# A hand-planned attention kernel: ScalarE planned by the pace of its ends, weights loaded later in pieces, any two neighbouring waiting score tiles in one exp, instruction lines asked for ahead

## The chip, the cores and the metric

The kernel runs on one core of a Trainium2 chip. The metric is device time in microseconds (us), the median of several executions; lower is better. TensorE is called PE here (its weight loads PEld), VectorE DVE, ScalarE ACT, GpSimd POOL, and SyncE, which only issues DMAs, SP. PSUM, where PE writes its results, has 8 banks, each 128 partitions by 512 fp32 numbers; they are numbered 0 to 7, and two banks are neighbours when their numbers differ by one.

## What is computed

```python
xn = layernorm(x)                                   # x: 2048 x 512, bf16
q  = (xn @ wq) as 32 heads of 16;  k = xn @ wk;  v = xn @ wv   # one k and v for all heads
s  = softmax(q @ k.T / 4) @ v, heads joined, @ wo   # no mask: every query sees every key
h  = silu(xn @ w1)                                  # 512 x 1792
g  = silu(h @ w2)                                   # 1792 x 512
out = x + s * g
```

## The kernel before, in words

**Work.** The 2048 queries are cut into 4 chunks of 512. Scores are made in *slots*: one slot is 2 heads by 64 keys by 512 queries, it fills one PSUM bank, and PE makes it with 4 matmuls of 64 x 32 weights (line 883). A *group* is 64 slots (4 heads of one chunk); there are 32 groups, so 2048 slots. Each slot's exponential is taken in one of two ways.

- An **A slot** is read by ACT with one exp (line 1578) into a place of `pa_sb`, which has NPA = 21 places. PE then multiplies it with v in 2 matmuls (line 1222). One ACTIVATE may read two slots, if their banks are neighbours and two places of `pa_sb` next to each other are free; this is called a *pair* below.
- A **D slot** is turned by DVE into 16-bit integers that are read as bf16 numbers (line 959), an approximate exponential. Four D slots make a batch; POOL adds three different constants to the integers of a whole batch (line 1144, three instructions for four slots), and PE multiplies all 4 versions with v, 8 matmuls for each slot (line 1222). The four weighted versions together make the approximation good enough.

The two MLP products run between the scores: 56 h jobs (w1, then a tanh on ACT at line 700 and a multiply on DVE at line 701) and 16 z jobs (w2, likewise); the q projections and 12 w jobs (wo; the last four row tiles have their own code at the end) follow the same path. PE works in two lanes of 4 matmuls each, whose row and column tiles don't overlap: scores go to lane 1, products with v to lane 0, and the jobs to whichever is free.

**What sets the order.** The whole order of every engine is written by a planner at build time, a loop that keeps one clock for each engine and always lets the engine with the earliest clock choose its next instruction. It uses a table of costs: `T_AF` (the fixed part of an ACTIVATE, beside 0.8333 ns for a column), `MM` (a round of 4 matmuls), `LAT` (from an engine's end to what another sees), and `FETCH` (the least time between two crossings of a line of 256 PE instructions). On the chip the engines follow these orders and wait on semaphores, so a wrong cost in the plan is not an error; it shows as one engine standing at a semaphore where the plan had it busy.

**Choices near the change.**

- `s_step` (line 1041) decides on lane 1 whether the next slot becomes an A or a D slot. It starts an A slot only while ACT's planned backlog `act_need()` is below `A_HIGH`, and a D slot only while DVE's, `dve_backlog()`, is below `D_HIGH`. `MARGIN` is the number of untouched slots that a group must still have for a new D batch.
- `best_a` (line 999) takes the bank of a new A slot: beside the *last* slot that waits for ACT, if that one has no mate.
- `act_step` (line 1547) chooses ACT's next instruction. It looks at the first `WIDE` = 2 of the waiting slots, in the order in which they were made, and reads both in one exp if both are visible within `PAIR_WAIT` and their banks are neighbours; else it reads the first alone.
- `tensor` (line 174) places a PE instruction. When it crosses a line of 256, it may not start before `FETCH` after the last crossing.
- Loads: SP issues x, wk, wv, wq, then all of w1 (1792 KB), w2 (1792 KB) and wo (512 KB) in the first 10 us (lines 424 to 426), and the rows of x that the output needs (`add_xr`, line 763).
- `can_start` (line 1282) and `start_jobs` (line 1297) start the h, z, q and w jobs by their due place (`pace`, in groups) and by the filling of `pa_sb`. Before xn of the first `4 * MIXJ` row tiles is placed, no such job starts (line 1306).
- D slots start when all 16 pieces of k are written (line 927); `take_ob` (line 1186) takes the bank in which a group's product with v is summed.

Of the kernel before, what the change touches and what calls it, by code (L numbers as in the profile page):

```python
# [18 lines left out]
LN_EPS = 1e-5  # L19
T_ISSUE, T_SWDGE = 450.0, 1000.0  # L20
J_BASE, J_END, MIXJ = 0.1, 1.0, 2
# [4 lines left out]
T_P, T_SH, T_TR, T_AF = 600.0, 600.0, 630.0, 52.0  # L26
T_P64, DV_MIN, T_LIB = 1015.0, 40, 300.0
HOLD_PO = 300.0
# [3 lines left out]
Q_URG = 1.153  # L32
J_SLIP = 1.193
NEXT_OB, OB_SLACK = 6, 500.0
NORM_PRIO, T_DIV = 0, 264.0
A_OPEN = 1
T_MS, V_AT = 500.0, 6
# [9 lines left out]
MM = 216.0  # L47
LINE, FETCH = 256, 3670.0
# [4 lines left out]
MARGIN, MARGIN_END = 23, 23  # L53
WIDE, PAIR_WAIT, GRP_WAIT = 2, 51.21, 348.513
Q_LEAD = 2.838
A_HIGH, D_HIGH, SLACK = 3164.101, 2393.829, 73.705
LEAD, CROWD, FRAG, DB_LOW = 427.04, 0.298, 4.106, 1
RUN, HOLD, PRESS = 6, 1017.195, 22
ROOM = 4
START_Z, START_H, AHEAD, NEAR = 10, 13, 1.45, 15  # L60
CLOSING, URGENT, END_DV = 7, 4.336, 60
STARVED = 561.894
JLATE, JEVAC = 1.901, 1
# [7 lines left out]
class Task:  # L71
# [11 lines left out]
    (PE, AC): 221.0, (PE, DV): 221.0, (PE, PE): SWAP,  # L83
    (AC, PE): 176.0, (AC, DV): 140.0, (AC, AC): 110.0, (AC, PO): 160.0, (AC, SP): 160.0,
# [6 lines left out]
class Planner:  # L91

    def __init__(self):
        self.clk = {e: 0.0 for e in ENGINES}
        self.order = {e: [] for e in ENGINES}
        self.lastw = {}
        self.readers = {}
        self.tasks = {e: [] for e in ENGINES}
        self.mode = None
        self.lane = [0.0, 0.0]  # L100
        self.fed, self.cross = 0, -INF
        self.dma_t = self.acc_t = 0.0
        self.count = 0
        self.last2 = {DV: None, PO: None}
# [69 lines left out]
    def tensor(self, mode, lane, dur, emit, reads, writes, t, after=None, n=8):  # L174
# [9 lines left out]
        if line > self.fed // LINE:  # L184
            t = max(t, self.cross + FETCH)
            self.cross = t
# [125 lines left out]
def bass_recurrent_scan__grouped_kv_mqa__dense_activation_silu__prompt_kernel(  # L312
# [29 lines left out]
    with ExitStack() as es:  # L342
# [50 lines left out]
        def bank(b):  # L393
            return ps[:, b * 512:(b + 1) * 512]
# [178 lines left out]
        def mk_K(c, ka, kb, bk=None):  # L573
# [13 lines left out]
            def consume(jb, op):  # L587
                b = jb.bank
                out = []
                for a in range(2):  # L590
                    dst = kt_sb[:, 0, a, ka * P:kb * P]
                    keys = [("kt", k, a) for k in range(ka, kb)]
                    held = [("ps", b), ("part", 0)]
                    if kb == 1:
                        t = Task(AC, T_AF + 93.0 + 0.8333 * n, lambda g, dst=dst, a=a: g.activation(
                            dst, bank(b)[:, 0:n], ACT.Copy, scale=part_sb[:, 0, a:a + 1]), held, keys, 0, out[-1:] or parts)
# [102 lines left out]
        def gated(b, k, scale, dst, key):  # L699
            t1 = Task(AC, 477.0, lambda a: a.activation(t_sb[:, k, :], bank(b), ACT.Tanh, scale=scale), [("ps", b)], [("t", k)], 0)  # L700
# [17 lines left out]
        def mk_z(tt, pace):  # L718
            c, r = divmod(tt, 4)

            def consume(jb, op):
# [10 lines left out]
                    lambda k, rows: w2_sb[rows, k, :], lambda k: ["w2", ("u", k)])  # L732
# [597 lines left out]
        def do_job(t, jb):  # L1330
            mk, rd, dur = jb.rounds[jb.pos]
            op = pl.tensor(jb.mode, None, dur, mk(jb.bank), rd, [("ps", jb.bank)], t)
# [158 lines left out]
        def pe_step():  # L1491
# [44 lines left out]
            if not t_done and ("ob", 3) in pl.lastw and pl.ready(PE, [("ob", 3)], [("ps", 6)]) <= t:  # L1536
                n = st["warm"] = st.get("warm", 0) + 1
                pl.tensor("F", None, T_COLD if n <= N_COLD else MM, lambda pe: pe.matmul(
                    bank(6), lhsT=zer_sb[:, 0:P], rhs=zer_sb[:, :], start=True, stop=True), [("ob", 3)], [("ps", 6)], t)
# [6 lines left out]

        def act_step():
# [138 lines left out]
```

## Time and profile before

| | before |
|---|---|
| median of 3 executions | 677.74 us (677.01 to 677.88) |
| the profiled execution | 678.45 us |
| its span, first to last instruction | 676.5 us |
| mean granted PE clock | 0.997 |
| largest busy shares | PE 98%, ACT 98%, DVE 93%, POOL 88% |

The profile lists for every engine its busy time and the number of its instructions; groups of instructions by line, with the number, the mean duration of one and what ended the idle time before them; the waits between engines in sum; a table by stretch of the span; and the chain of work that ended last. A duration in the groups reaches from an instruction's start to its own end, and on ACT one instruction starts before the last has ended, so the mean duration (745 ns for a single exp) is not the pace at which they follow each other; that pace is read from the chain, where consecutive pieces of one engine are laid end to end. Likewise PE's busy share is no measure of its load, since matmuls overlap; matmuls per us of a stretch are.

### The profile page before, as it was taken

What the parts mean: (1) busy time and instruction counts of PE and PEld (TensorE: products, weight loads), DVE (VectorE), ACT (ScalarE), POOL (GpSimd) and SP (SyncE); (2) the same over time, 40 slices, a digit from 0 to 9 for tenths busy, and PEclk for the clock granted to TensorE, in tenths of its full rate; (3) what the DMA queues carried; (4) which work ended last, traced back from release to release, by engine and by line L of the source; (5) the groups of instructions that cost most, each with busy time, mean ns of one, the idle gap of its engine ahead of it and who ended that gap; (6) DMA issues with size and microseconds to landing.
All of it is one profiled execution on the core that took longest, in us unless ns stands there. A gap on an engine that the chain in (4) does not pass through costs nothing.

```text
span 676.5 us, 47198 instructions
## 1 busy us (share of the span) xinstructions
PE 666.1 (98%) x21990; PEld 324.4 (48%) x21990; DVE 631.4 (93%) x1144; ACT 659.8 (98%) x1198; POOL 598.2 (88%) x596
## 2 busy tenths in 40 slices
PE   7999999999999999999999999999999999999997
PEld 3445455444444444445344455554445545454443
DVE  8889999999999999998999999999899999999972
ACT  5999999999999999999999999999999999999995
POOL 4028899999989999998999998999799999999981
PEclk9999999999999999999999999999999999999999
DMA  8510000000000000000000000000000001000001
GB/s 298 170 31 4 5 4 5 4 5 4 5 4 21 19 29 12 5 4 5 4 5 4 21 27 28 5 4 5 4 5 4 5 20 36 19 5 5 5 4 34
DMA packets 11733, 14.98 MB, mean 22 GB/s; under 512 B 1809, under 2 KB 10769, under 8 KB 11537
## 3 DMA queue, kind: packets, MB, share of 16 engines
q1 hardware_dynamic: 10928, 10.78, 5.0%
q8 instruction: 172, 2.82, 1.7%
q0 software_dynamic: 320, 0.92, 0.5%
q10 hardware_dynamic: 288, 0.26, 0.1%
q14 instruction: 25, 0.20, 0.1%
HBM read 8.95 MB, written 2.10 MB: 16 GB/s over the span
## 4 chain that ended last, share of the span: by engine, by line
PE 61%; ACT 34%; DVE 3%; issue 0%
PE ps L883 34%; ACT pa_sb L1578 32%; PE ps L652 13%; PE ps L1222 12%; ACT t_sb L700 2%; DVE stats_sb L486 1%; PE ps L1429 0%; PE ps L554 0%; DVE kt_sb L598 0%; DVE xnT_sb L565 0%; DVE xn_sb L515 0%; PE ps L580 0%; DVE v_sb L626 0%; PE ps L617 0%; DVE var_sb L509 0%
## 5 line engine op out<-in xcount | busy, mean ns | idle before, releaser
L1578 ACT ACTIVATE pa_sb<-ps 128x512 bf16<-128x512 f32 (+1 forms) x1107 | 633.5, 804 | 4.6 <-PE ps L883 4.0
L1144 POOL INT64_ADD ds_sb<-db_sb x580 | 589.0, 1039 | 29.5 <-PE ps L1222 16.3
L883 PE MATMUL ps<-qt_sb,kt_sb 64*32 64x512 bf16 x8192 | 566.4, 380 | 3.9 <-ACT pa_sb L1578 1.2
L959 DVE TENSOR_SCALAR db_sb<-ps 128x512 uint16<-128x512 f32 x776 | 487.0, 682 | 17.7 <-PE ps L883 9.9
L1222 PE MATMUL ps<-ds_sb,v_sb 64*32 64x512 bf16 x4656 | 409.5, 377 | 0.0
L883 PEld LDWEIGHTS ps<-qt_sb,kt_sb 64*32 64x32 bf16 x8192 | 184.4, 90 | 267.0 <-ACT pa_sb L1578 163.1
L1222 PE MATMUL ps<-pa_sb,v_sb 64*32 64x512 bf16 x2544 | 308.9, 379 | 0.0
L1222 PE MATMUL ps<-db_sb,v_sb 64*32 64x512 bf16 x1552 | 190.2, 378 | 0.0
L1222 PEld LDWEIGHTS ps<-ds_sb,v_sb 64*32 64x32 bf16 x4656 | 146.3, 91 | 11.6 <-issue 0.6
L652 PE MATMUL ps<-xnT_sb,w_sb 64*32 64x512 bf16 x1792 | 135.7, 378 | 0.1
L652 PE MATMUL ps<-w_sb,u_sb 64*32 64x512 bf16 x1792 | 133.9, 378 | 0.0
L1222 PEld LDWEIGHTS ps<-pa_sb,v_sb 64*32 64x32 bf16 x2544 | 89.0, 91 | 9.5 <-ACT pa_sb L1578 2.7
L1222 PEld LDWEIGHTS ps<-db_sb,v_sb 64*32 64x32 bf16 x1552 | 55.7, 91 | 4.6
L700 ACT ACTIVATE t_sb<-ps 128x512 bf16<-128x512 f32 x72 | 53.1, 737 | 0.0
L652 PEld LDWEIGHTS ps<-xnT_sb,w_sb 64*32 64x32 bf16 x1792 | 42.3, 91 | 17.5 <-ACT pa_sb L1578 2.9
L652 PEld LDWEIGHTS ps<-w_sb,u_sb 64*32 64x32 bf16 x1792 | 43.0, 91 | 14.0 <-DVE db_sb L959 0.8
L701 DVE SCALAR_TENSOR_TENSOR u_sb<-t_sb,ps 128x512 bf16<-128x512 bf16 x56 | 38.0, 678 | 1.0 <-ACT t_sb L700 0.5
L652 PE MATMUL ps<-xnT_sb,wq_sb 64*32 64x512 bf16 x480 | 37.7, 378 | 0.0
L1239 DVE STREAM_TRANSPOSE ps<-ps 128x512 f32<-128x512 f32 (+1 forms) x33 | 23.2, 707 | 13.0 <-PE ps L1222 13.0
L652 PE MATMUL ps<-wo_sb,on_sb 64*32 64x512 bf16 x384 | 31.6, 378 | 0.1
L1268 POOL DMA_DIRECT2D kt_sb<-kt_sb x4 | 2.8, 699 | 27.2 <-DVE mv_sb L490 10.1
L1244 DVE TENSOR_TENSOR otr_sb<-ps,rcp_sb 128x256 bf16<-128x256 f32 (+1 forms) x33 | 13.3, 404 | 0.2
(73 smaller groups left out, 182.6 us busy)
## 6 DMA issues: line engine op xcount, KB each, us to landing
w_sb<-in_B_w_dram SPq DMA_DIRECT2D x2, 1792.0 KB, 13.8
xr_sb<-in_A_x_dram SPq DMA_DIRECT2D x16, 128.0 KB, 2.9
out_dram<-ob_sb SPq DMA_DIRECT2D x16, 128.0 KB, 1.8
ds_sb<-in_A_x_dram SPq DMA_DIRECT2D x3, 512.0 KB, 6.8
kt_sb<-kt_sb POOLq DMA_DIRECT2D x4, 224.0 KB, 2.9
wq_sb<-in_A_wq_dram SPq DMA_DIRECT2D x1, 512.0 KB, 4.9
wo_sb<-in_A_wo_dram SPq DMA_DIRECT2D x1, 512.0 KB, 16.9
ds_sb<-in_A_x_dram SPq DMA_DIRECT2D x2, 128.0 KB, 3.0
```

Source lines behind the costliest of these rows:

```text
L486: ts_ = pl.add(Task(DV, 593.0, lambda v, t=t: v.bn_stats(stats_sb[:, t, :], x_tile(t)), [xkey(t)], [("st", t)], 1 + j, gate=(lambda j=j: S ...
L652: h = pe.matmul(bank(b)[32 * j:32 * (j + 1), :], lhsT=lhs(k, rows, 32 * j, 32), rhs=rhs(k, rows), start=first, stop=last, tile_position=(r ...
L700: t1 = Task(AC, 477.0, lambda a: a.activation(t_sb[:, k, :], bank(b), ACT.Tanh, scale=scale), [("ps", b)], [("t", k)], 0)
L701: t2 = Task(DV, T_P, lambda v: v.scalar_tensor_tensor(out=dst, in0=t_sb[:, k, :], scalar=1.0, in1=bank(b), op0=ALU.add, op1=ALU.mult), [(" ...
L883: h = pe.matmul(bank(b)[32 * j:32 * j + 32, :], lhsT=kt_sb[r0:r0 + 64, g % 2, i, k0:k0 + 32], rhs=qt_sb[r0:r0 + 64, g // 2 % NQR, :], star ...
L959: bt.P[k] = pl.add(Task(DV, T_P, lambda v: v.tensor_scalar(db_sb[:, bt.b, k * NQ:(k + 1) * NQ], bank(b), 128.0 * LOG2E, 128.0 * (SHIFT_BET ...
L1144: whole["po"].append(pl.add(Task(PO, T_P64, lambda g: g.int64_add(ds_sb[:, s, :].bitcast(U64), db_sb[:, bt.b, :].bitcast(U64), words), rea ...
L1222: h = pe.matmul(bank(OB)[q:q + 32, :], lhsT=lhs[rows], rhs=rhs[rows], start=s0, stop=s1, tile_position=(64 * l, q), skip_group_check=True)
L1239: t1 = pl.add(Task(DV, (T_TR - 60.0) / parts + 60.0, lambda v, cols=cols: v.transpose(bank(OB)[:, cols], bank(OB)[:, cols]), [("ps", OB)], ...
L1244: norm["m", g, h] = pl.add(Task(DV, T_DIV / parts + 68.0, lambda v, bl=bl: v.tensor_tensor(o3[:, bl, DH * e:DH * e + DH], f3[:, bl, 0:DH], ...
L1268: kt1[c] = pl.add(Task(PO, T_SWDGE, lambda e: e.dma_start(kt_sb[DH:P, 1, :, cols], kt_sb[0:P - DH, 0, :, cols]), [("kt", k, a) for k in ra ...
L1578: op = pl.place(AC, 0.8333 * NQ * n + T_AF, lambda a: a.activation(pa_sb[:, s * NQ:(s + n) * NQ].rearrange("p (b n) -> p b n", n=NQ), ps3[ ...
```

## The change

The diff does five things, and sets some forty numbers of the planner anew.

1. **Costs.** `T_AF` becomes 63.5, the three places that had costs of their own for ACT use it, `MM` becomes 218, some latencies are changed.
2. **Lines.** A crossing waits for the line's arrival (`come`). A line is asked for when PE is `LOOK` = 68 instructions short of the line before it, and comes `FETCH` after that or after the line before. Jobs count their true number of instructions.
3. **Loads.** w1 is issued behind xn of row tile 5; w2 in four pieces, each behind one of the first h results; wo and the first rows for the output behind later ones.
4. **Pairs.** `best_a` looks for a bank beside *any* waiting slot without a mate; `act_step` pairs any slot that is visible with a neighbour that is visible, out of order, unless the oldest has waited more than `SKIP` = 1500 ns.
5. **Numbers.** Among others `A_HIGH` 3164 to 1583, `D_HIGH` 2394 to 1518, `MARGIN` 23 to 19, `MIXJ` 2 to 3, `PRESS` 22 to 18.

```diff
+W1_AT, SKIP = 5, 1500.0
-J_BASE, J_END, MIXJ = 0.1, 1.0, 2
+J_BASE, J_END, MIXJ = 0.073, 1.084, 3
-T_P, T_SH, T_TR, T_AF = 600.0, 600.0, 630.0, 52.0
+T_P, T_SH, T_TR, T_AF = 600.0, 600.0, 630.0, 63.5
-HOLD_PO = 300.0
+HOLD_PO = 374.374
...
-MM = 216.0
-LINE, FETCH = 256, 3670.0
+MM = 218.0
+LINE, FETCH, FED, LOOK = 256, 3684.358, 58, 68
...
-MARGIN, MARGIN_END = 23, 23
-WIDE, PAIR_WAIT, GRP_WAIT = 2, 51.21, 348.513
+MARGIN, MARGIN_END = 19, 20
+WIDE, PAIR_WAIT, GRP_WAIT = 14, 47.267, 237.034
-A_HIGH, D_HIGH, SLACK = 3164.101, 2393.829, 73.705
+A_HIGH, D_HIGH, SLACK = 1582.599, 1518.392, 43.301
-RUN, HOLD, PRESS = 6, 1017.195, 22
-ROOM = 4
-START_Z, START_H, AHEAD, NEAR = 10, 13, 1.45, 15
+RUN, HOLD, PRESS = 6, 1411.229, 18
+ROOM = 5
+START_Z, START_H, AHEAD, NEAR = 8, 9, 1.03, 17
...
-    (AC, PE): 176.0, (AC, DV): 140.0, (AC, AC): 110.0, (AC, PO): 160.0, (AC, SP): 160.0,
+    (AC, PE): 154.0, (AC, DV): 135.0, (AC, AC): 110.0, (AC, PO): 160.0, (AC, SP): 160.0,
...
         if line > self.fed // LINE:
-            t = max(t, self.cross + FETCH)
-            self.cross = t
+            t = max(t, self.come[line])
+        ahead = (self.fed + n + LOOK) // LINE
+        if ahead == len(self.come) - 1:
+            self.come.append(max(t, self.come[ahead]) + FETCH)
...
-        dma(SP, "w1", w1_sb[:], B_w1.rearrange("(dc p) f -> p dc f", p=P), 1792, ["w1"], prio=2)
-        dma(SP, "w2", w2_sb[:], B_w2.rearrange("(ft p) n -> p ft n", p=P), 1792, ["w2"], prio=3)
-        dma(SP, "wo", wo_sb[:], A_wo.rearrange("(o p) n -> p o n", p=P), 512, ["wo"], prio=4)
+        def later(task, which):
+            task.gate = lambda: which() is not None and which().op is not None
+            task.after = lambda: which().op
...
+        later(dma(SP, "w1", w1_sb[:], w1v, 1792, ["w1"], prio=2), lambda: xn_task.get(W1_AT))
+        for k, (f0, f1) in enumerate(((0, 4), (4, 8), (8, 11), (11, 14))):
+            later(dma(SP, "w2", w2_sb[:, f0:f1, :], w2v[:, f0:f1, :], 128 * (f1 - f0), [("w2", k)], prio=3), hidden(0, k))
+        wov = A_wo.rearrange("(o p) n -> p o n", p=P)
+        later(dma(SP, "wo", wo_sb[:], wov, 512, ["wo"], prio=4), hidden(0, 4))
...
-            t1 = Task(AC, 477.0, lambda a: a.activation(t_sb[:, k, :], bank(b), ACT.Tanh, scale=scale), [("ps", b)], [("t", k)], 0)
+            t1 = Task(AC, T_AF + 0.8333 * NQ, lambda a: a.activation(t_sb[:, k, :], bank(b), ACT.Tanh, scale=scale), [("ps", b)], [("t", k)], 0)
...
+            if tt < 4:
+                later(xr_task[tt], hidden(0, 5))
...
         def best_a(banks, when):
-            u = units[-1] if len(units) > st["expn"] else None
-            if u is not None and not u.mate:
-                near = [b for b in banks if abs(b - u.bank) == 1]
-                if near:
-                    return min(near, key=lambda b: room(when) - room([x for x in when if x != b])), True
+            lone = {u.bank: u for u in units[st["expn"]:] if not u.mate}
+            near = [b for b in banks if b - 1 in lone or b + 1 in lone]
+            if near:
+                b = min(near, key=lambda b: room(when) - room([x for x in when if x != b]))
+                lone[b - 1 if b - 1 in lone else b + 1].mate = True
+                return b, True
...
+        def waiting(t):
+            q = units[st["expn"]:]
+            if not q:
+                return q
+            q = [u for u in q if u.vis <= max(t, q[0].vis) + PAIR_WAIT]
+            at = {u.bank: u for u in q}
+            for u in q:
+                if u is not q[0] and t - q[0].vis > SKIP:
+                    break
+                near = [at[b] for b in (u.bank - 1, u.bank + 1) if b in at]
+                if near:
+                    return [u, min(near, key=lambda v: q.index(v))]
+            return q[:1]
 
         def act_step():
...
-            q = units[st["expn"]:st["expn"] + WIDE]
+            q = waiting(t)
             rx = None
             if q:
-                q.sort(key=lambda u: u.bank) if False else None
-                q = [u for u in q if u.vis <= max(t, q[0].vis) + PAIR_WAIT]
-                while len(q) > 1:
-                    bs = sorted(u.bank for u in q)
-                    if bs[-1] - bs[0] == len(q) - 1:
-                        break
-                    q.pop()
...
             if rx is not None and rx <= t + 25:
+                for u in q:
+                    units.remove(u)
                 q.sort(key=lambda u: u.bank)
+                units[st["expn"]:st["expn"]] = q
```

More of the change, by code (lines that the diff above doesn't have):

```diff
@@ L24 @@
 LOG2E = 1.4426950408889634
[L26 removed]
+T_P, T_SH, T_TR, T_AF = 600.0, 600.0, 630.0, 63.5
 T_P64, DV_MIN, T_LIB = 1015.0, 40, 300.0
[L28 removed]
+HOLD_PO = 374.374
 RSQRT_M = float(0x5F1FFFF9)
 RSQRT_C = ((-0.703952253, 0.703952253 * 2.38924456), (-0.5, 1.5))
[L32 to L34 removed]
+Q_URG = 0.308
+J_SLIP = 1.308
+NEXT_OB, OB_SLACK = 6, 192.595
 NORM_PRIO, T_DIV = 0, 264.0
[L36 to L37 removed]
+A_OPEN = 5
+T_MS, V_AT = 500.0, 7
 T_TP, T_COLD, N_COLD = 56.0, 427.0, 11
@@ L100, in __init__ @@
         self.lane = [0.0, 0.0]
-        self.fed, self.cross = 0, -INF
+        self.fed, self.come = FED, [-INF, -INF]
         self.dma_t = self.acc_t = 0.0
@@ L731, in mk_z @@
             product(jb, lambda k, rows, a, n: u_sb[rows, k, r * P + a:r * P + a + n],
-                    lambda k, rows: w2_sb[rows, k, :], lambda k: ["w2", ("u", k)])
+                    lambda k, rows: w2_sb[rows, k, :], lambda k: [("w2", (k >= 4) + (k >= 8) + (k >= 11)), ("u", k)])
         def scaled(tt, b, r=None):
@@ L1331, in do_job @@
             mk, rd, dur = jb.rounds[jb.pos]
-            op = pl.tensor(jb.mode, None, dur, mk(jb.bank), rd, [("ps", jb.bank)], t)
+            op = pl.tensor(jb.mode, None, dur, mk(jb.bank), rd, [("ps", jb.bank)], t,
+                           n={"F": 2 * NDC * len(jb.arg) if jb.kind == "T" else 8, "H": 64}.get(jb.mode, 8))
             jb.pos += 1
@@ L1538, in pe_step @@
                 pl.tensor("F", None, T_COLD if n <= N_COLD else MM, lambda pe: pe.matmul(
-                    bank(6), lhsT=zer_sb[:, 0:P], rhs=zer_sb[:, :], start=True, stop=True), [("ob", 3)], [("ps", 6)], t)
+                    bank(6), lhsT=zer_sb[:, 0:P], rhs=zer_sb[:, :], start=True, stop=True), [("ob", 3)], [("ps", 6)], t, n=2)
                 return True
```

17 lines of the change are left out of this document (10 added, 7 removed).

## The prediction, made before the changed kernel was run

> **What bounds the kernel now.** I read the header and the shares first. Four engines are nearly full at once, so the table by stretch comes next, to see whether that holds in each stage or only on average; then the groups, for the number of instructions of each kind.
>
> ```profile
> span 676.5 us, 47198 instructions
> PE 666.1 (98%) x21990; PEld 324.4 (48%) x21990; DVE 631.4 (93%) x1144; ACT 659.8 (98%) x1198; POOL 598.2 (88%) x596
> ```
>
> ```profile
> 0.00:17.00 17.00, 13.10 (x239) 6.48 (x243) 14.63 (x78) 9.63 (x19) 7.24 (x13) 0.96 0.90 298
> 17.00:34.00 17.00, 15.99 (x369) 7.72 (x357) 14.56 (x39) 15.86 (x27) 0.66 (x1) 0.94 0.54 168
> 34.00:51.00 17.00, 16.74 (x458) 8.45 (x450) 14.37 (x32) 16.16 (x29) 5.04 (x6) 1.00 0.11 31
> 51.00:100.00 49.00, 48.89 (x1662) 26.05 (x1662) 48.39 (x84) 49.00 (x92) 44.47 (x45) 1.00 0.02 5
> 100.00:200.00 100.00, 99.64 (x3416) 47.79 (x3396) 96.56 (x163) 99.98 (x185) 96.89 (x96) 1.00 0.02 5
> 200.00:300.00 100.00, 99.99 (x3452) 46.11 (x3443) 98.37 (x168) 99.86 (x182) 98.03 (x98) 1.00 0.05 15
> 300.00:400.00 100.00, 99.59 (x3384) 48.08 (x3384) 94.56 (x161) 100.00 (x188) 95.42 (x95) 1.00 0.04 10
> 400.00:500.00 100.00, 99.53 (x3384) 50.17 (x3360) 94.46 (x160) 99.78 (x187) 94.18 (x94) 1.00 0.04 10
> 500.00:600.00 100.00, 99.87 (x3424) 50.59 (x3416) 96.78 (x165) 100.00 (x180) 97.70 (x97) 1.00 0.05 15
> 600.00:640.00 40.00, 40.00 (x1370) 18.01 (x1352) 38.88 (x66) 40.00 (x77) 39.45 (x40) 1.00 0.02 5
> 640.00:660.00 20.00, 20.00 (x662) 9.28 (x656) 15.15 (x25) 20.00 (x31) 16.70 (x17) 1.00 0.02 4
> ```
>
> The columns are stretch, length, then PE, PEld, DVE, ACT, POOL with busy us and number of instructions, the clock, DMA share and GB/s. From 51 to 660 us ACT is busy in every microsecond but a few tenths; DVE and POOL have 2 to 6% left. PE's busy share says nothing, but its count does: 1662 + 3416 + 3452 + 3384 + 3384 + 3424 + 1370 + 662 = 20,754 matmuls in 609 us, 29.34 ns for each, and in its best stretch (200 to 300) 100 us / 3452 = 28.97 ns. The best is only 1.3% ahead of the mean, so PE runs close to a pace of its own.
>
> ```profile
> L1144 POOL INT64_ADD ds_sb<-db_sb x580 | 589.0, 1039 | 29.5 <-PE ps L1222 16.3 <-PE ps L883 9.3 <-DVE db_sb L959 3.3
> L883 PE MATMUL ps<-qt_sb,kt_sb 64*32 64x512 bf16 x8192 | 566.4, 380 | 3.9 <-ACT pa_sb L1578 1.2 <-issue 1.0 <-DVE v_sb L626 0.4
> L1578 ACT ACTIVATE pa_sb<-ps 128x512 bf16<-128x512 f32 x942 | 502.9, 745 | 2.1 <-PE ps L883 1.7
> L959 DVE TENSOR_SCALAR db_sb<-ps 128x512 uint16<-128x512 f32 x776 | 487.0, 682 | 17.7 <-PE ps L883 9.9 <-PE ps L1222 3.5 <-POOL ds_sb L1144 0.8
> L1222 PE MATMUL ps<-ds_sb,v_sb 64*32 64x512 bf16 x4656 | 409.5, 377 | 0.0
> L1222 PE MATMUL ps<-pa_sb,v_sb 64*32 64x512 bf16 x2544 | 308.9, 379 | 0.0
> L1222 PE MATMUL ps<-db_sb,v_sb 64*32 64x512 bf16 x1552 | 190.2, 378 | 0.0
> ...
> L1578 ACT ACTIVATE pa_sb<-ps 128x1024 bf16<-128x1024 f32 x165 | 182.0, 1145 | 2.5 <-PE ps L883 2.3
> ```
>
> The slots are split into 942 + 2 x 165 = 1272 A slots and 776 D slots. An A slot costs PE 4 + 2544/1272 = 6 matmuls, a D slot 4 + (4656 + 1552)/776 = 12. Only 330 of the 1272 A slots share an exp.
>
> How long an exp really holds ACT is in the chain, whose pieces lie end to end:
>
> ```profile
> 349.30 1.83 ACT pa_sb L1578 x2
> 351.13 0.49 ACT t_sb L700
> 351.62 1.47 ACT pa_sb L1578 x3
> 353.09 0.49 ACT t_sb L700
> 353.58 2.45 ACT pa_sb L1578 x5
> ```
>
> Five singles take 2.45 us, 0.49 each; the two of the first row are pairs, 1.83/2 = 0.915 each. So a pair saves 2 x 0.49 - 0.915 = 0.065 us, and I use 0.063, from 0.49 against 512 columns at (0.915 - 0.49)/512 = 0.83 ns: 0.49 - 0.427. The plan before had 0.427 + 0.052 = 0.479 for a single, so it believed ACT 11 ns faster at each of some 1180 instructions, and PE pays for it by standing at banks that ACT has not left yet:
>
> ```profile
> PEld ps L883 <- ACT pa_sb L1578: 163.1, 573, 0.7
> ...
> ACT pa_sb L1578 <- PE ps L883: 4.0, 6, 2.0
> ```
>
> PE's score loads wait 573 times for an exp (163.1 us of the load queue, much of it beside running matmuls), ACT only 6 times for PE. ACT is the bound, PE the second, and PSUM banks are what they meet at.
>
> **The change part by part.** *Pairs* (`waiting`, `best_a`). At least none is added (165 stay); at most all 1272 slots pair, 636. Saving S on ACT: 0 to 471 x 0.063 = 29.7 us. For: half of the 1107 exps end with a score standing behind them, and a pair frees two neighbours at one instant, which then are refilled together. Against: 8 banks, of which the sum and a job take about two and the D slots some more. `D_HIGH` falls by 0.88 us, more than one D slot of 0.68, so about one bank passes to the A slots. Reading out of order also lets the oldest slot stand for up to 1.5 us; what waits for it is its product with v, and at a group's end the sum, so it costs only there: 32 groups, nothing as long as the next group's products are at hand. No row lies near either end, so I take the middle, 400 pairs: S = 235 x 0.063 = 14.8 us.
>
> The Trainium skill, page "ScalarE: Activation LUTs", section "What ACT_TABLE_LOAD costs", gives an ACTIVATE with immediates a fixed 186 ns, of which 93 ns overlap with the next, so 93 ns would go with each pair; by that S would be an estimated 21.9 us. The chain shows 63 ns, and the sum keeps it.
>
> *Costs and lines.* They add no instruction; they change where in PE's order scores, products and jobs stand. With ACT's true pace in the plan PE should be put before a bank that is free. Gain P: nothing, up to PE holding its best stretch's pace in all stretches, 20,754 x (29.34 - 28.97) ns = 7.7 us. Below nothing there is no end of P's own: PE that waits more is the last rival. I take 7.7, since a whole 100 us of the same mixture ran at that pace, with the most D work beside it.
>
> *How S and P become time.* Let d slots go from D to A (which `A_HIGH`, `D_HIGH` and `MARGIN` decide). ACT pays 0.458 us for each (half a pair), PE is spared 6 x 29.34 ns = 0.176 us. With x saved, ACT gives x = S - 0.458 d and PE x = P + 0.176 d. So x = (0.176 S + 0.458 P) / 0.634 = (2.60 + 3.53)/0.634 = **9.7 us**, with d = 11. POOL loses 11 x 0.75 x 1.04 = 8.6 us and DVE 11 x 0.6 = 6.6 of work, about as much as the span, so neither becomes the bound. The ends: S = P = 0 gives 0, S = 29.7 with P = 7.7 gives 13.8.
>
> *Loads.* Which waits could they touch?
>
> ```profile
> w_sb<-in_B_w_dram SPq DMA_DIRECT2D x2, 1792.0 KB, 13.8
> ...
> ds_sb<-in_A_x_dram SPq DMA_DIRECT2D x3, 512.0 KB, 6.8
> ...
> wo_sb<-in_A_wo_dram SPq DMA_DIRECT2D x1, 512.0 KB, 16.9
> ```
>
> ```profile
> 16.21 1.38 DVE L515 TENSOR_SCALAR xn_sb<-ds_sb,mv_sb,rstd_sb 128x512 bf16<-128x512 bf16 x4
> ...
> 27.70 1.05 DVE L515 TENSOR_SCALAR xn_sb<-ds_sb,mv_sb,rstd_sb 128x512 bf16<-128x512 bf16 x3
> ...
> 57.30 0.69 DVE L701 SCALAR_TENSOR_TENSOR u_sb<-t_sb,ps 128x512 bf16<-128x512 bf16 x1
> ```
>
> ```profile
> L652 PE MATMUL ps<-xnT_sb,w_sb x1792: 372/376/388, 22.9 to 582.7; 64*32 64x512 bf16 x200
> ...
> L652 PE MATMUL ps<-w_sb,u_sb x1792: 375/376/388, 106.9 to 657.1; 64*32 64x512 bf16 x200
> ```
>
> w1 behind xn of tile 5 (about 17 us) lands about 31; the first h started at 22.9, but with `MIXJ` = 3 it waits for tile 11 (28.7) anyway, so w1 delays it 2 us more. That moves one or two h jobs of 56 behind the opening, where PE does 369 matmuls in 17 us against 576 at its mean pace: cost nothing, at most two jobs of 32 matmuls, 1.9 us. The four w2 pieces leave behind the first h results; SP then stands at these waits, and behind it on its queue wait the other pieces, wo, the four rows of x and much later the stores. In this trace four h results were there at 58 us, and a piece of 512 KB takes 6.8 us, while the first z is at 106.9: some 40 us of cover. If it were gone, z and its tanh would be late, and other jobs would fill in.
>
> What the pieces may disturb is PE's own instruction supply, which now meets them in the full stretch:
>
> ```profile
> q8 instruction: 172, 2.82, 1.7%
> ```
>
> ```profile
> PEld ps L883 <- issue: 2.6, 8, 0.6
> PEld ps L652 <- issue: 2.6, 7, 0.6
> ...
> PEld ps L1222 <- issue: 0.6, 2, 0.4
> ```
>
> 2.82 MB in 172 packets is 16.4 KB each, one for 43,980/172 = 256 PE instructions. The waits of 51 to 660 us that nothing visible ends are 5.8 us in 17 pieces. Six more loads at most double the longest, 0.6 us, at each: 3.6 us lost, or, since the opening is relieved of 4 MB, something gained. I take 0.
>
> *Ends.* D slots start after the last k. `MIXJ` = 3 takes h work out of DVE's way before that, POOL's first add is at 47 us; the last z may come some tenths earlier. Within 3 us either way; I take 0.
>
> **Sum.** 678.45 - 9.7 = 668.75 on the profiled execution, which lies 0.71 above the median: **668.0 us**.
>
> **The rivals.**
> 1. *PE has room.* If its pace is not its own but ACT's, as the 573 waits say, PE gives way and all of S counts: 677.7 - 14.8 = 663, with more pairs down to 655. For it: ACT is full in all stretches. Against: matmuls per 100 us hardly vary, 3384 to 3452, and there are waits on nothing visible. The Trainium skill, page "Runtime: NRT & Kernel Launch", section "Instruction fetch mechanics", is on its side: fetching is hidden, since instructions leave more slowly than blocks of 256 come. By that the lines would be worth nothing and hold PE back nowhere. The waits of 0.6 us speak against it in part.
> 2. *PE stays as slow as it is.* P = 0: x = 2.60/0.634 = 4.1, 673.6 us. The same place is reached by few new pairs with P whole: 3.53/0.634 = 5.6, 672.
> 3. *It doesn't do what it says.* No bank beside a waiting slot is free, pairs stay near 165, the plan's mistakes elsewhere fill up: 677.7.
> 4. *Slower: ACT starves behind its pairs.* A pair holds two banks for 0.915 us and returns both at once; then two scores at 0.22 us a round, each 0.38 long, must be made before the next pair can be read, with a backlog cut to 1.58 us. ACT's 4.0 us of waiting would grow. The turning point is a mean wait of 14.8/400 = 0.037 us behind each pair. At 0.1 us ACT loses 40 - 14.8 = 25.2 us; shared with PE by the formula (P = 0) that is 0.278 x 25.2 = 7.0: 685 us. Against it: ACT almost never waits today.
>
> **How the numbers follow.** Forecast (666 to 672) 0.42, PE has room 0.25, PE stays 0.17, no effect 0.05, starving 0.11. A measurement of this kernel can tell about 0.2%, 1.4 us. Faster 0.84, same 0.05, slower 0.11. Range 655.0 to 677.0: below it part of the first rival, above it the last two.
>
> **What would show it.** Right: some 400 instructions of 128x1024 at line 1578; A slots near 1283; ACT's waits for PE under 10 us; over 3450 matmuls in each 100 us; fewer than 573 waits for exps. Wrong: pairs under 250; ACT idle by tens of us after pairs; issue waits grown between 45 and 90 us; POOL's first add later than 50 us.

## The result and the profile after

| | before | changed |
|---|---|---|
| median | 677.23 us (676.50 to 678.13, 22 executions) | 674.58 us (671.38 to 677.95, 22 executions) |
| ratio | 1 | 0.9961, interval 0.9951 to 0.9971 |
| the profiled execution | 678.45 us, span 676.5 | 674.70 us, span 672.9 |

So the change is faster by 0.39%, 2.65 us, where 9.7 us were forecast. The direction was right, the size was not: the sum was more than three times too large. The medians also differ in another way, to which the last experiments lead: the changed kernel's executions lie 6.6 us apart, those of the kernel before 1.6.

The changed kernel's shares, its table by stretch and its groups, which answer to the same views of before:

```profile
span 672.9 us, 47414 instructions
PE 660.8 (98%) x22086; PEld 373.0 (55%) x22086; DVE 632.6 (94%) x1158; ACT 653.9 (97%) x1172; POOL 612.1 (91%) x610
```

```profile
100.00:200.00 100.00, 99.87 (x3460) 58.69 (x3451) 98.81 (x169) 99.39 (x183) 99.95 (x99) 1.00 0.02 5
200.00:300.00 100.00, 99.99 (x3500) 55.85 (x3499) 99.62 (x172) 99.90 (x179) 99.17 (x99) 1.00 0.05 15
300.00:400.00 100.00, 99.92 (x3454) 54.37 (x3441) 96.87 (x167) 99.99 (x181) 99.00 (x98) 1.00 0.04 10
400.00:500.00 100.00, 100.00 (x3471) 60.55 (x3461) 96.95 (x167) 99.74 (x183) 97.83 (x98) 1.00 0.04 10
500.00:600.00 100.00, 99.52 (x3442) 56.06 (x3431) 98.03 (x168) 99.33 (x182) 100.00 (x99) 1.00 0.05 15
600.00:640.00 40.00, 39.69 (x1388) 23.46 (x1380) 38.37 (x66) 39.49 (x74) 38.01 (x39) 1.00 0.02 5
640.00:660.00 20.00, 19.02 (x576) 9.04 (x556) 5.96 (x11) 20.00 (x29) 15.96 (x16) 1.00 0.01 3
660.00:672.90 12.90, 7.43 (x150) 2.51 (x138) 4.71 (x13) 5.67 (x9) 0.00 (x0) 1.00 0.13 43
```

PE runs 3442 to 3500 matmuls in each 100 us, before 3384 to 3452. POOL, 94 to 98% busy before, has reached 98 to 100. From 640 us DVE does little (5.96 of 20 us, before 15.15), while ACT is full.

```profile
L1160 POOL INT64_ADD ds_sb<-db_sb x594 | 602.8, 1044 | 12.8 <-DVE db_sb L974 6.2 <-PE ps L1238 4.8 <-PE ps L898 1.6
...
L974 DVE TENSOR_SCALAR db_sb<-ps 128x512 uint16<-128x512 f32 x792 | 493.2, 680 | 10.8 <-PE ps L898 5.9 <-POOL ds_sb L1160 2.0 <-PE ps L1238 1.0
L1605 ACT ACTIVATE pa_sb<-ps 128x512 bf16<-128x512 f32 x906 | 477.5, 694 | 4.9 <-PE ps L898 4.5
...
L1605 ACT ACTIVATE pa_sb<-ps 128x1024 bf16<-128x1024 f32 x175 | 183.0, 1096 | 2.0 <-PE ps L898 1.6
```

Here is where the sum fails: **175 pairs** instead of 400, before 165. A slots are 906 + 2 x 175 = 1256, sixteen fewer than before, not eleven more; D slots are 792. ACT was relieved, by 16 x 0.427 + 26 x 0.063 = 8.5 us, but by giving slots away.

```profile
PEld ps L898 <- ACT pa_sb L1605: 81.9, 336, 0.8
PEld ps L898 <- DVE db_sb L974: 30.4, 136, 0.5
DVE ps L1255 <- PE ps L1238: 16.8, 4, 13.6
```

The score loads wait for exps half as long as before (163.1 us, 573 times), as forecast. Other signs that I had named for a right forecast came too: ACT's exps wait 6.1 us for scores, under 10, and four of the five stretches of 100 us have over 3450 matmuls. But pairs under 250 were a sign of being wrong. DVE's longest wait, in one piece at the end of the span, is 13.6 us; before it was 8.0:

```profile
DVE ps L1239 <- PE ps L1222: 13.0, 7, 8.0
```

The chain of the changed kernel shows what it waits for (start, us, what):

```profile
639.54 9.06 ACT pa_sb L1605 x15
648.60 0.49 ACT t_sb L713
649.09 13.33 ACT pa_sb L1605 x15
662.42 0.04 issue
662.46 0.40 PE ps L1238 x4
```

ACT's exps set the last 23 us before the closing work. DVE has read its last D slot at 644.2 us, before at 657.2; POOL's adds for the D slots go on until 656.0 (the changed kernel's lines, then the one of before):

```profile
643.47 0.69 DVE L974 TENSOR_SCALAR db_sb<-ps 128x512 uint16<-128x512 f32 x1 [0.30 <-PE ps L1238]
638.64 17.33 POOL L1160 INT64_ADD ds_sb<-db_sb  x17 [0.40 <-PE ps L898]
```

```profile
655.27 1.89 DVE L959 TENSOR_SCALAR db_sb<-ps 128x512 uint16<-128x512 f32 x3 [0.71 <-PE ps L883]
```

### The profile page after: what moved, and what is told of

It reads as the page before. It is cut to its first block, busy times and chain, and to the rows that moved or that the text cites. A ratio compares the mean times of both kernels' runs of the same rounds, so it can differ in the third digit from the quotient of the medians.

```text
span 672.9 us, 47414 instructions
## 1 busy us (share of the span) xinstructions
PE 660.8 (98%) x22086; PEld 373.0 (55%) x22086; DVE 632.6 (94%) x1158; ACT 653.9 (97%) x1172; POOL 612.1 (91%) x610
## 4 chain that ended last, share of the span: by engine, by line
PE 74%; ACT 20%; DVE 4%; POOL 1%; issue 0%
PE ps L898 31%; PE ps L1238 26%; ACT pa_sb L1605 19%; PE ps L665 16%; DVE stats_sb L499 1%; ACT t_sb L713 1%; DVE xn_sb L528 1%; POOL kt_sb L461 1%; PE ps L1446 0%; DVE kt_sb L611 0%; DVE xnT_sb L578 0%; DVE v_sb L639 0%; POOL v_sb L459 0%; DVE var_sb L522 0%; DVE var_sb L524 0%
## 5 line engine op out<-in xcount | busy, mean ns | idle before, releaser
L1605 ACT ACTIVATE pa_sb<-ps 128x512 bf16<-128x512 f32 (+1 forms) x1081 | 622.8, 759 | 6.9 <-PE ps L898 6.1
L1160 POOL INT64_ADD ds_sb<-db_sb x594 | 602.8, 1044 | 12.8 <-DVE db_sb L974 6.2
L974 DVE TENSOR_SCALAR db_sb<-ps 128x512 uint16<-128x512 f32 x792 | 493.2, 680 | 10.8 <-PE ps L898 5.9
L1238 PE MATMUL ps<-pa_sb,v_sb 64*32 64x512 bf16 x2512 | 330.7, 377 | 3.0 <-ACT pa_sb L1605 2.3
L898 PEld LDWEIGHTS ps<-qt_sb,kt_sb 64*32 64x32 bf16 x8192 | 197.6, 90 | 190.0 <-ACT pa_sb L1605 81.9
L1238 PEld LDWEIGHTS ps<-ds_sb,v_sb 64*32 64x32 bf16 x4752 | 166.7, 92 | 22.0 <-issue 3.4
L665 PE MATMUL ps<-w_sb,u_sb 64*32 64x512 bf16 x1792 | 140.1, 378 | 0.5 <-issue 0.5
L1238 PEld LDWEIGHTS ps<-pa_sb,v_sb 64*32 64x32 bf16 x2512 | 101.6, 92 | 25.1 <-ACT pa_sb L1605 11.1
L665 PEld LDWEIGHTS ps<-w_sb,u_sb 64*32 64x32 bf16 x1792 | 48.8, 92 | 12.8 <-issue 2.6
L1284 POOL DMA_DIRECT2D kt_sb<-kt_sb x4 | 2.8, 700 | 23.8 <-DVE kt_sb L611 14.6
L665 PEld LDWEIGHTS ps<-xnT_sb,wq_sb 64*32 64x32 bf16 x480 | 11.7, 91 | 4.1 <-DVE db_sb L974 0.7
```

Source lines behind the costliest of these rows:

```text
L665: h = pe.matmul(bank(b)[32 * j:32 * (j + 1), :], lhsT=lhs(k, rows, 32 * j, 32), rhs=rhs(k, rows), start=first, stop=last, tile_position=(r ...
L898: h = pe.matmul(bank(b)[32 * j:32 * j + 32, :], lhsT=kt_sb[r0:r0 + 64, g % 2, i, k0:k0 + 32], rhs=qt_sb[r0:r0 + 64, g // 2 % NQR, :], star ...
L974: bt.P[k] = pl.add(Task(DV, T_P, lambda v: v.tensor_scalar(db_sb[:, bt.b, k * NQ:(k + 1) * NQ], bank(b), 128.0 * LOG2E, 128.0 * (SHIFT_BET ...
L1160: whole["po"].append(pl.add(Task(PO, T_P64, lambda g: g.int64_add(ds_sb[:, s, :].bitcast(U64), db_sb[:, bt.b, :].bitcast(U64), words), rea ...
L1238: h = pe.matmul(bank(OB)[q:q + 32, :], lhsT=lhs[rows], rhs=rhs[rows], start=s0, stop=s1, tile_position=(64 * l, q), skip_group_check=True)
L1605: op = pl.place(AC, 0.8333 * NQ * n + T_AF, lambda a: a.activation(pa_sb[:, s * NQ:(s + n) * NQ].rearrange("p (b n) -> p b n", n=NQ), ps3[ ...
```

## The experiments

Each ratio is to the kernel before, run beside it on the same chip; the chips differ, so the ratios compare better than the times. Where a kernel's number of pairs and A slots is given, it is counted in its program. The kernels of one session were measured beside each other: the four parts on one chip; those on pairs, loads and the end on a second; PE by itself, more_instructions, costs_numbers and other_lead on a third; after_again and the three on lines on that third chip too, but later; the last two on a fourth.

**The parts, one at a time and one left out.** My theory A held that the true costs bring the gain through PE's order; rival B, that the forty numbers do.

only_costs, and its opposite no_costs, which is the changed kernel with these lines as before:

```diff
-T_P, T_SH, T_TR, T_AF = 600.0, 600.0, 630.0, 52.0
+T_P, T_SH, T_TR, T_AF = 600.0, 600.0, 630.0, 63.5
-MM = 216.0
+MM = 218.0
-    (AC, PE): 176.0, (AC, DV): 140.0, (AC, AC): 110.0, (AC, PO): 160.0, (AC, SP): 160.0,
+    (AC, PE): 154.0, (AC, DV): 135.0, (AC, AC): 110.0, (AC, PO): 160.0, (AC, SP): 160.0,
```

> The kernel before with the planner's costs alone corrected (T_AF, MM, the latencies, the three ACT costs). It has 178 pairs and 1268 A slots, before 165 and 1272. Theory A (the gain is PE's order under true costs): P is there almost whole, S is 13 x 0.063 = 0.8 us, so (0.176 x 0.8 + 0.458 x 8)/0.634 = 6, less some us at the end of the span: 672 to 674.5 us; the score loads wait for exps under 120 us in sum, before 163. Rival B (the gain is the forty numbers): within 1 us of before, 677, and the waits as before.

Measured: 1.0026, interval 1.0014 to 1.0038: slower. The score loads do wait less for exps, 91.4 us, but that isn't time.

> The changed kernel with the planner's costs as before (T_AF 52, MM 216, old latencies); all else of the change stays. 152 pairs, 1260 A slots. Theory A: the gain goes, 676 to 678 us, and the score loads wait for exps over 130 us in sum. Rival B: it stays, 674 to 675 us.

Measured: 1.0008, 0.9992 to 1.0025. The gain isn't there, though the score loads wait 117.2 us for exps, not over 130.

only_numbers and no_numbers, the lines of the diff that set numbers alone:

```diff
-A_HIGH, D_HIGH, SLACK = 3164.101, 2393.829, 73.705
+A_HIGH, D_HIGH, SLACK = 1582.599, 1518.392, 43.301
...
```

> The kernel before with the planner's forty numbers of the change alone (A_HIGH, D_HIGH, MARGIN, MIXJ and so on), the costs, lines, loads and pairs as before. 126 pairs, 1264 A slots. Theory A: no gain, 677 us within 1.5. Rival B: most of the gain, 674 to 675 us.

Measured: 1.0011, 1.0001 to 1.0022.

> The changed kernel with the forty numbers as before; costs, lines, loads and pairs of the change stay. 173 pairs, 1260 A slots. Theory A: the gain stays, 673 to 675 us. Rival B: it goes, 677 us.

Measured: 1.0044, 1.0027 to 1.0061.

As measured, both A and B fall: neither part alone is a gain, and without either one the rest is none. The changed kernel itself was not measured on this chip, and after_again below shows that it does not gain on every occasion, so this is not proof. That numbers and costs are fitted to each other is my guess; no_numbers, with the costs of the change and the numbers of before, is the slowest of the four. POOL's idle time before its adds is 24.1, 19.9, 26.1 and 24.1 us in these four, 29.5 before and 12.8 in the changed kernel; but two later executions of the changed kernel have 18.3 and 14.8, so it is no sure mark of it.

One thing mars the kernels that take the numbers without the new pair rule (only_numbers and, below, costs_numbers and costs_numbers_lines). `WIDE` = 14, which the new `act_step` doesn't use, lets the old one read longer runs: 6, 6 and 9 of their exps read three slots.

**Pairs.** no_pairs_at_all and wait_for_mate are the changed kernel with one line each:

```diff
-                near = [at[b] for b in (u.bank - 1, u.bank + 1) if b in at]
+                near = []
```

> The changed kernel with each A slot read by its own exp: 0 pairs, 1248 A slots, 800 D slots. S is -175 x 0.063 = -11.0 us against the changed kernel. By the formula of the prediction with P unchanged: 0.278 x 11.0 = 3.1 us slower, 677.7. If ACT alone set the time: 11.0 less the 8 slots fewer (3.9), 7.1 us slower, 681.7. If pairs were worth nothing (PE or GpSimd the bound): within 1 us of 674.6.

Measured: 1.0036, 1.0019 to 1.0053, against 0.9961 for the changed kernel: 0.75% or some 5 us slower, between the 3.1 of the formula and the 7.1 of ACT alone. On this same chip no_loads has 0.9974 and longer_end 0.9965, whose orders are the changed kernel's, or are it up to the last group; against these it is 4 to 5 us. The 175 pairs are worth their place. (The profiled execution, 674.75 us, was the fastest of its twelve; no size is read from it.)

```diff
-WIDE, PAIR_WAIT, GRP_WAIT = 14, 47.267, 237.034
+WIDE, PAIR_WAIT, GRP_WAIT = 14, 250.0, 237.034
```

> The changed kernel in which ACT waits up to 250 ns for a neighbour instead of 47 (PAIR_WAIT): 282 pairs, 1240 A slots. If only the number of pairs counted, S grows by 107 x 0.063 = 6.7 us: 672.5 us. If pairs can only be had by standing still, each bought pair costs up to 0.25 us of ACT and saves 0.063: up to 107 x 0.19 = 20 us of ACT, shared 0.278 x 20 = 5.6 or more: 680 us or slower, and ACT's waits for PE grow by tens of us.

Measured: 1.0137, 1.0121 to 1.0153: 686.71 us, slower by 1.4% than before, with 282 pairs. ACT pays for them by standing, 18.5 us ahead of the pairs, where the changed kernel has 2.0:

```profile
L1605 ACT ACTIVATE pa_sb<-ps 128x512 bf16<-128x512 f32 x676 | 358.3, 633 | 1.4 <-PE ps L898 1.0
...
L1605 ACT ACTIVATE pa_sb<-ps 128x1024 bf16<-128x1024 f32 x282 | 285.6, 1046 | 18.5 <-PE ps L898 12.4 <-PE ps L1238 1.1 <-PE ps L665 0.2
```

A pair beyond those that come by themselves costs more than the 0.063 us it saves. This is the mechanism of my fourth rival, though the change doesn't set it off, because it waits 47 ns at most.

**Loads.** no_loads issues the weights in the first 10 us again; all compute orders stay the same, so this is the cleanest pair of kernels here.

```diff
-        later(dma(SP, "w1", w1_sb[:], w1v, 1792, ["w1"], prio=2), lambda: xn_task.get(W1_AT))
+        dma(SP, "w1", w1_sb[:], B_w1.rearrange("(dc p) f -> p dc f", p=P), 1792, ["w1"], prio=2)
...
```

> The changed kernel with all weights loaded in the first 10 us again; every compute engine's order is the same as in the changed kernel, only SP's differs. Theory A: the place of the loads is worth nothing, within 1 us of the changed kernel (674.6). Rival C (the late pieces disturb PE's instruction supply): faster by 1 to 3.6 us, and the load queue's waits on nothing visible smaller by as much between 30 and 100 us.

Measured: 0.9974, 0.9958 to 0.9989. The interval overlaps the changed kernel's; the later loads are worth nothing that can be told, as I took. The load queue's waits on nothing visible between 30 and 100 us are 1.4 us, 2.9 in the changed kernel: that half of rival C is there, but it doesn't become time.

**The end.** longer_end:

```diff
-MARGIN, MARGIN_END = 19, 20
+MARGIN, MARGIN_END = 19, 12
```

> The changed kernel with MARGIN_END 12 in place of 20: one more batch of D slots in the last group, 4 A slots fewer; the order is the same up to the last group. If the end is lost because ACT reads alone while DVE is done (13.6 us of DVE waiting at the end), ACT is spared 4 x 0.46 = 1.8 us: 672.8 us. If GpSimd, busy to 656 us, bounds the end, the batch's three adds cost 3.1 us there: 674.6 or slower.

Measured: 0.9965, 0.9947 to 0.9982. Undecided: the 1.8 us would be 0.27%, and the interval is wider. The second branch wasn't put to the test at all: POOL has 594 adds as in the changed kernel, since the planner gave the added batch's three to DVE (line 1156, 1.9 us).

**PE by itself.** lines_alone leaves all work out; PE runs 16,384 matmuls with no wait at all, two lanes as in the kernel:

```python
for k in range(1024):                     # 4 stages: 512, 512, 256, 256 columns
    l, b = k % 2, k % 8
    for j in range(4):
        r0 = 64 * (j // 2 ^ l)
        h = pe.matmul(ps[32 * j:32 * (j + 1), b * 512:b * 512 + n], lhsT=lhs_sb[r0:r0 + 64, j, :],
                      rhs=rhs_sb[r0:r0 + 64, 0:n], start=True, stop=True, tile_position=(r0, 32 * j), ...)
```

> A kernel of its own, which leaves all the work out and stores zeros: PE alone runs 16,384 matmuls of 64 x 32 weights in the two lanes, without any wait: 4096 with 512 columns, 4096 the same while 512 KB loads run one after another at their start, then 4096 and 4096 with 256 columns, alone and with loads. Theory S (PE's instruction supply is a bound of its own): with 256 columns the pace doesn't double; it stays near 28 ns for a matmul, 3.6 us for 256 instructions. With 512 columns it is near the same. Rival (the array is the bound, supply hidden): 27 ns with 512 columns, 14 to 20 ns with 256. Loads that disturb the supply would show as a slower pace in the stretch in which they run.

Measured: with 512 columns (first row; columns PE, PEld, DVE, POOL with busy us and count, then clock, DMA share, GB/s), with 256 columns (the second and third):

```profile
160.00:200.00 40.00, 39.44 (x1424) 22.56 (x1411) 0.00 (x0) 0.00 (x0) 1.00 0.02 5
...
240.00:260.00 20.00, 11.64 (x768) 10.36 (x768) 0.00 (x0) 0.00 (x0) 1.00 0.02 5
260.00:300.00 40.00, 21.34 (x1408) 19.00 (x1408) 0.00 (x0) 0.00 (x0) 1.00 0.02 5
```

40 us / 1424 = 28.1 ns for a matmul with 512 columns, and 60 us / (768 + 1408) = 27.6 ns with half of them: the number of columns hardly matters. The timeline of the 256-column stage shows why:

```profile
250.72 1.94 PE L39 MATMUL ps<-rhs_sb,lhs_sb 64*32 64x256 bf16 x128 [1.53 <-issue]
254.19 1.94 PE L39 MATMUL ps<-rhs_sb,lhs_sb 64*32 64x256 bf16 x128 [1.53 <-issue]
```

After every 128 matmuls and their loads, 256 instructions, PE stands 1.53 us on nothing that the profile shows; the period is 254.19 - 250.72 = 3.47 us. Elsewhere in this stage and the next it is mostly 3.7 to 4.0, in part at a lower granted clock (0.87 in the row of 300 to 340 us). So with 256 columns PE is held by the supply of its instructions, and the array is not the bound: theory S holds for its pace with 256 columns. With 512 columns, which the kernel has, PE hardly stands; hundreds of matmuls follow each other:

```profile
117.62 11.01 PE L39 MATMUL ps<-rhs_sb,lhs_sb 64*32 64x512 bf16 x385
128.99 11.26 PE L39 MATMUL ps<-rhs_sb,lhs_sb 64*32 64x512 bf16 x400 [0.35 <-issue]
```

There array and supply come out at nearly the same pace, and this run can't tell which of them binds. The four loads of 512 KB, from 122.8 to 134.0 us, made no difference: 721 matmuls in the 20 us from 120, 712 and 728 in the 20 us before and behind.

more_instructions puts this to the test inside the changed kernel:

```diff
                     r0, k0 = 64 * (j // 2 ^ 1), 64 * kb + 32 * (j % 2)
+                    if kb % 2 == 0 and j == 0:
+                        pe.matmul(bank(b)[0:32, 0:16], lhsT=kt_sb[r0:r0 + 64, g % 2, i, k0:k0 + 32], ...)
```

> The changed kernel with a matmul of 16 columns put ahead of every other score slot's first matmul, 1024 in all, overwritten by what follows: 2048 more PE instructions, 8 lines of 256, next to no work for the array. The order is otherwise the same. Theory S: up to 8 x 3.66 = 29 us slower where lines bind all along; 10 to 29, 685 to 703 us. Rival (PE has room, ACT and GpSimd are the bound): under 4 us, 675 to 678.5 us.

Measured: 1.0285, 1.0245 to 1.0324: 19 us over the kernel before beside it, 698.88 against 679.63, some 3.2% or 22 us over the changed kernel by the ratios, 11 ns for each added instruction, of which 2048 at 3.47 us for 256 would be 28. My first rival, "PE has room", put it under 4 us and is out. Its load queue's waits on nothing visible (51 to 660 us) are 38.5 us, 13.6 in the changed kernel; in part:

```profile
PEld ps L1242 <- issue: 16.1, 36, 0.8
...
PEld ps L902 <- issue: 13.4, 29, 0.9
```

Where these waits stand says what they are: all 89 of them, and all 36 of the changed kernel, come at the 91st to 93rd weight load when the loads are counted off by 128, that is at one place in each 256 instructions. The added matmuls could also have cost time in the array; but the waits at this place grew by 24.9 us, and the spans of the two profiled executions differ by 26.8.

**What the gain needs.** After A and B had fallen, theory D held that costs and numbers together do it, through POOL.

> The kernel before with the corrected costs and the forty numbers, without the changes of lines, loads and pairs: 125 pairs, 1252 A slots, 796 D slots. Theory D (the two together let GpSimd take more D slots without standing idle): the gain is there, 674 to 676 us, GpSimd's idle time between its adds under 12 us (24.8 before, 7.6 in the changed kernel, 17 to 23 with one of the two alone). Rival (all parts are needed, or the gain is one lucky order): 677 us or slower.

Measured: 0.9997, 0.9975 to 1.0019, POOL idle 20.0 us. Costs and numbers together aren't enough; that POOL's idle time makes the gain is neither shown nor refuted. On the same chip, the changed kernel with another lead of the q projections:

```diff
-Q_LEAD = 4.233
+Q_LEAD = 4.3
```

> The changed kernel with one number moved that says nothing of the engines' load: Q_LEAD, the lead of a q projection, 4.3 groups in place of 4.233. 149 pairs, 1252 A slots. It is another order of the same kind. If the gain comes from what the change does: 673 to 676 us, and GpSimd's idle time under 12 us. If the gain is one lucky order out of many: back at 677 or above.

Measured: 0.9956, 0.9934 to 0.9979, 676.59 us, POOL idle 15.7 us over the span (12.2 from 51 to 660). By the times neither branch is met, since the kernel before took 679.63 here; by the ratio the gain is there. An order that differs in chance only keeps it, so it isn't one lucky order.

Then the lines, beside the changed kernel itself. no_lines has the old rule, costs_numbers_lines has three parts of the diff, lines_never_bind has this:

```diff
-LINE, FETCH, FED, LOOK = 256, 3684.358, 58, 68
+LINE, FETCH, FED, LOOK = 256, 3550.0, 58, 68
```

> The changed kernel once more, beside the next three. Every theory: a ratio of about 0.996 to the kernel before, as in the first measurement; if executions on another chip move it by more than 0.3%, the differences found so far between single parts are no larger than that.

Measured: **0.9998**, 0.9970 to 1.0026, 675.59 to 683.83 us.

> The changed kernel with the planner's lines as before (no earlier crossing than 3670 ns after the last one); costs, loads, pairs and numbers of the change. 151 pairs, 1256 A slots. If the lines are the missing part: ratio 0.999 to 1.002. If they are not: 0.995 to 0.997.

Measured: 0.9997, 0.9975 to 1.0019.

> The kernel before with costs, numbers and lines of the change, its loads and pairs as before. 134 pairs, 1252 A slots. If the lines are the missing part: ratio 0.994 to 0.998, as the changed kernel. If not: 0.999 to 1.002, as costs with numbers.

Measured: 0.9984, 0.9965 to 1.0003.

> The changed kernel with FETCH 3550 in place of 3684 ns: in the plan a line always comes in time. 163 pairs, 1248 A slots, 800 D slots. If the plan must know how slowly lines come: ratio 0.999 or worse, and more waits on nothing visible. If it is enough that it doesn't hold PE back: 0.994 to 0.997.

Measured: 0.9986, 0.9963 to 1.0010.

Beside these the changed kernel has no gain, so nothing can be said there of what the gain needs. The chip alone is not the reason, since other_lead had its 0.9956 on the same one. costs_numbers_lines is also the changed kernel without its pair rule, as the loads change no compute engine's order; it is no slower than after_again, so nothing shows that the rule earns anything.

But the same program, once in 674.7 and once in 681.0 us (spans 672.9 and 679.2), is a comparison of its own. First the changed kernel's row of 51 to 640 us and its waits on nothing visible (51 to 660), then the same of after_again:

```profile
51.00:640.00 589.00, 587.18 (x20312) 338.16 (x20304) 576.13 (x985) 585.79 (x1066) 579.72 (x572) 1.00 0.05 14
```

```profile
PEld ps L1238 <- issue: 5.8, 17, 0.7
...
PEld ps L665 <- issue: 4.3, 8, 1.1
PEld ps L898 <- issue: 3.5, 11, 0.7
```

```profile
51.00:640.00 589.00, 584.17 (x20096) 344.36 (x20092) 572.28 (x975) 582.57 (x1054) 574.24 (x566) 1.00 0.05 14
```

```profile
PEld ps L1238 <- issue: 13.9, 34, 0.7
...
PEld ps L665 <- issue: 6.2, 14, 1.3
PEld ps L898 <- issue: 5.0, 13, 0.7
```

216 matmuls fewer in the same 589 us, 216 x 29.2 ns = 6.3 us, all of the difference of the spans. The load queue's waits on nothing visible are 25.1 us against 13.6, all 61 of them at the 91st to 93rd load of 128 again; the score loads' waits for exps went down, 56.7 us against 81.9 over the span. One kernel, one order, one clock (1.00 in both rows): PE got its instructions more slowly.

> The changed kernel a third time. Theory S (the supply of PE's instructions sets what of the gain arrives): the ratio to before lies between 0.996 and 1.000, its executions spread over 5 us or more, and the profiled one has waits on nothing visible (51 to 660 us) near 14 us if it takes about 674.5 us and near 25 if about 681. Rival (the second measurement was a stray): 0.995 to 0.997 again, with a spread under 4 us.

Measured: 0.9965, 0.9950 to 0.9979, 672.21 to 676.81 us; its profiled execution, 676.41 us, has 13.4 us of such waits at the load queue. This decides nothing: the ratio fits both, the spread of 4.6 us neither, and the waits are as few as in the execution of 674.70 us, though this one took 1.7 us longer.

> The changed kernel with Q_LEAD 4.3 a second time. Theory S: within 0.3% of the changed kernel beside it, whatever that is. Rival (each order has its own time): the same 0.9956 as before, apart from the changed kernel if that moves.

Measured: 0.9952, 0.9934 to 0.9971, 0.13% from the changed kernel beside it. As that one had its gain here, both branches are met and nothing is decided. Between the two profiled executions of this program lies a second pair like the one above: 23.8 us of such waits with a span of 675.3 us, now 15.1 with 672.3. Three of the changed kernel's measurements and its twin's two are thus 0.9961, 0.9998, 0.9965, 0.9956 and 0.9952: a gain of 0.4% as a rule, nothing on one occasion.

## Why the prediction was wrong, point by point

1. **S, the saving by pairs, is the step that failed.** I took 400 pairs, the middle between 165 and 636, with no row behind it. There are 175, S = 10 x 0.063 = 0.6 us instead of 14.8, and that alone takes the sum from 9.7 to (0.176 x 0.6 + 0.458 x 7.7)/0.634 = 5.7 us. The argument was that half of the exps end with a score standing behind them. That is a sign of *few* waiting slots, not of many: a score that stands before a bank hasn't been made yet. Pairs need slots that wait for ACT in neighbouring banks, and the traces, read with the banks in the programs, show that such slots are hardly ever there. From 51 to 660 us, 863 exps of the changed kernel read one slot. When these start, another A slot is finished and unread at 165 of them, and in a neighbouring bank at 2; before it was 175 and 4 of 895. Even if slots that are finished 0.2 us later count, a neighbour is there at 74 of the 863. ACT reads the slots almost as fast as they are made, so there is little to pair, and a wider search finds little more. That waiting for pairs doesn't pay is shown by wait_for_mate.
2. **P came out near its size, in part by luck.** The row of before for 51 to 640 us; the changed kernel's stands above:

```profile
51.00:640.00 589.00, 587.51 (x20006) 286.81 (x19998) 568.00 (x961) 588.61 (x1084) 566.14 (x559) 1.00 0.04 10
```

   Before 20,006 matmuls, after 20,312: 29.44 and 29.00 ns, over 20,312 matmuls 8.9 us against 7.7 forecast, which I had called the upper end. (The forecast's mean of 29.34 ns added up rows, each of which also counts the matmuls that straddle its borders; the one row of 51 to 660 us has 20,654, 29.49 ns.) But the size belongs to this execution: the same program has 29.10 ns in after_third and 29.31 in after_again, 6.9 and 2.6 us by the same working. And the cause that I gave it, true costs, isn't shown: only_costs doesn't gain.
3. **The formula fits this execution once S and P are measured.** x = (0.176 x 0.6 + 0.458 x 8.9)/0.634 = 6.6 us and d = (0.6 - 6.6)/0.458 = -13: slots go from A to D. Measured are d = -16 and 3.6 us of span. P is taken from the same trace, so the test is d alone. My second rival named this place, few pairs with P whole, at 672 us.
4. **The end, which I took at 0, cost 3.3 us.** The last row of before is:

```profile
660.00:676.50 16.50, 12.76 (x302) 5.66 (x286) 4.70 (x13) 9.50 (x14) 2.42 (x3) 1.00 0.10 35
```

   At 640 us the kernel before has 662 + 302 = 964 matmuls left, the changed one 576 + 150 = 726. That is 238 x 29.2 ns = 6.9 us ahead, against 6.6 by the formula, and 3.6 remain. Some 1.1 us of the lead are from the opening, which I had at 0 too: 1088 matmuls in the first 51 us, 1050 in the kernel before, whose granted clock was 0.97 there against 1.00. The chain shows ACT's exps there; longer_end leaves open whether more D slots would have helped.
5. **"Neither becomes the bound" was wrong for POOL**, as far as its busy time tells: d had the other sign, and 14 more adds bring it to 100% in two stretches.
6. The loads at 0: right, as far as can be told. The slower rival: not set off, its mechanism real.

So the step that failed is S, the 400 pairs, and the end at 0 is the next in size. What stays open is which parts of the change the 0.4% need. Parts alone and parts left out came within 0.5% of before, mostly where the changed kernel wasn't measured beside them or had no gain itself; the pair rule was never measured alone, and left out only where the changed kernel had no gain.

## What to carry to other kernels

A saving that needs two things at the same place and time must have a row that shows how often both are there; the middle between "never" and "always" is no estimate. When four engines are full at once, write the balance down as equations, as here, and ask of each new work split which engine it fills. And when two versions differ by half a per cent, measure each on more than one occasion and beside the other: here one program moved by 0.4% against the same partner.

## What was not expected of the hardware

PE, fed with 64 x 32 tiles of 256 columns, is bound by the supply of its instructions: 3.47 us at best for 256, which leaves 27 ns for a matmul with its load, though the matmuls themselves take 1.94 us for 128. With 512 columns it runs at 28.1 ns, nearly the same pace, so for a kernel like this one the run doesn't tell the two bounds apart. But in the kernels' traces, too, the waits that nothing visible ends come at one place in each 256 instructions only. The Trainium skill, page "Runtime: NRT & Kernel Launch", section "Instruction fetch mechanics", says that fetching is hidden; the rows of lines_alone, 1.53 us of standing after each 256 instructions, differ, and the measurement decides. While a store of 2 MB ran in that kernel (its issue is at 369.5 us), the period was once 6.8 us:

```profile
372.39 1.94 PE L39 MATMUL ps<-rhs_sb,lhs_sb 64*32 64x256 bf16 x128 [1.80 <-issue]
379.15 6.03 PE L39 MATMUL ps<-rhs_sb,lhs_sb 64*32 64x256 bf16 x256 [4.82 <-issue]
```

379.15 - 372.39 = 6.76 us. It happened once; that the store did it isn't shown. The spread between executions of one program comes in part from this supply: in two pairs of executions the slower one has more such waits, 25.1 us against 13.6 and 23.8 against 15.1, with spans 6.3 and 3.0 us longer. It isn't all of it, as after_third shows. And that a kernel which runs closer to this supply spreads more is not shown: the kernel before spread over 1.6 us in the first measurement, but over 6.3 us beside after_again.
